# Eleven half-size products for twelve in the MLP's first matrix multiply, with shared parts added in PSUM

## The chip, the cores and the metric

The kernel runs on one core of one Trainium2 chip. The metric is the device time of one execution in microseconds. The five engines of a core are called PE (TensorE, matrix multiply), DVE (VectorE), ACT (ScalarE), POOL (GpSimd) and SP (SyncE, which here issues DMAs). Each works through its own instructions in order; they wait for each other through semaphores.

## The reference

A delta-rule attention makes tokens, and these go through an MLP with a hard-swish. All is fp32 in its results; the two MLP weights arrive as fp64.

```python
# attention: B, H, S, D = 4, 8, 768, 48
k_n = k / (norm(k) + 1e-6)
for t in range(S):
    y[:, :, t] = q_t @ state
    v_old = state^T k_t
    state = state + beta_t * outer(k_t, v_t - v_old)
# MLP: x is y as (B*S, H*D) = (3072, 384); w_in (384, 2048); w_out (2048, 384)
h = x @ w_in
g = h * np.clip(h + 3.0, 0.0, 6.0) / 6.0
return g @ w_out
```

## The kernel before

**Attention.** The sequence is cut into 24 chunks of 32 positions, for the 4 batches at once: 128 tokens a chunk. A chunk t has a preparation (`prep`, six chunks ahead: GpSimd normalises k into kb and makes the mask mb, PE transposes k and q, `pt`, and makes the scores, `sc`; DVE masks them into LB; GpSimd scales kb into bkb) and a chain (`chain`: state products `ks`, L775; R on DVE, L788; `pz`; the state's update `su`; the output `py`; the transposed output `yt`, which ACT copies into `xT`). Every four chunks a group of triangular matrices is inverted on DVE (`inverse`, L719 and L724: 60 small steps, each with two inputs in SBUF), and the norms of a later group are made (`norms`: GpSimd squares, DVE reduces).

**MLP.** Two chunks are a block of 256 tokens; there are 12 blocks. `up` makes x @ w_in for the 16 tiles of 128 features: three products of 128x128 weights with 256 token columns into one PSUM bank (L946), then ACT makes Relu(h/6 + 1/2) into a buffer t1 (L955) and DVE makes min(t1, 1) * h into g (L958). Block 0 is done in two halves of 128 columns, as each chunk's tokens arrive. Blocks 0 and 1 multiply by w_out plainly (`down`, L987). From block 2 on `down_by_seven` (L1052) uses Strassen's seven products, each of 8 feature tiles with 192 columns, done in two halves of four products. Its sums of g, 16 of 128x256 a block, are on DVE (L1038), spread over the products; the sums of w_out were made once.

**Order.** Nothing is scheduled by the tile framework; the code's own order is the order of each engine. Up to chunk 4 it is the list of words in `ORDER` (each word advances one generator by a step; `u` is a unit of the MLP, `i2` a step of an inverse). From chunk 5 on a loop gives each chunk 15 slots: in a slot come the chunk's planned steps, one MLP unit, then `settle`, which issues ACT's steps and all but one of DVE's final steps that are outstanding, then two or three steps of an inverse or of norms. A block has 14 units of `down_by_seven` and 16 of `up`, so two chunks' slots hold one block. After the last chunk the remaining MLP units run alone.

**Buffers.** PSUM has four banks shared by the MLP and the attention's small products (`psM`) and four for the chain (`psC`). kb has 2 buffers, bkb and LB 8, v 3, mb 2.

## Time and profile before

| | us |
|---|---|
| median of 3 runs (lowest, highest) | 699.43 (697.33, 704.33) |
| the profiled execution | 701.2 |
| its span | 699.5 |
| DVE, sums of g (L1038), 160 | 65.5 busy |
| DVE, final steps of 256 columns (L958), 176 | 73.3 busy |
| ACT, Relu of 256 columns (L955), 176 | 83.5 busy |
| GpSimd, mask steps of 128x256 (L423), 48 | 35.8 busy |
| chunk 7 begins (its `ks`), chunk 9 begins | 234.47, 286.44 |

A line of the profile names the source line, the engine, the operation and what it reads and writes (out<-in), with the partitions by the elements of a partition. PEld is the loading of weights into PE, which goes on beside PE's products. An fp32 product appears as two records of PE, and so does its weight load.

### The profile page before, as it was taken

How to read it: one execution, taken by the hardware profiler on the slowest of the kernel's cores; microseconds unless marked ns; L12 is line 12 of the kernel's file. 1: busy time of each engine (PE TensorE's matmuls, PEld its weight loads, DVE VectorE, ACT ScalarE, POOL GpSimd, SP SyncE). 2: the span in 40 equal slices, each digit the busy share in tenths (PEclk: the TensorE clock that was granted, in tenths of full speed). 3: DMA queues.
4: the chain of work that ended last, by engine and by line, in shares of the span. 5: the costliest groups of instructions: out<-in, count | busy, mean ns of one | idle time of the engine just before them, and what ended most of it. 6: DMA issues, size and time to landing. Idle time of an engine off the chain costs nothing.

```text
span 699.5 us, 25481 instructions
## 1 busy us (share of the span) xinstructions
PE 651.9 (93%) x11208; PEld 570.9 (82%) x11208; DVE 440.0 (63%) x1174; ACT 240.6 (34%) x476; POOL 93.5 (13%) x146
## 2 busy tenths in 40 slices
PE   2637779999999999999999999999999999999997
PEld 2437669777668998998998998988988989989997
DVE  5678737878545797653796743895544984545342
ACT  5786448722213313313213213223223132132230
POOL 7520110321321010411100401100000000000000
PEclk9857859999999999999999999999999999999999
DMA  6787777401513123414113422015130014000000
GB/s 134 213 195 196 115 210 173 67 33 20 104 39 80 34 43 70 48 39 88 32 29 78 45 45 65 10 42 78 18 70 2 2 36 59 16 11 1 24 0 23
DMA packets 137999, 45.27 MB, mean 65 GB/s; under 512 B 128192, under 2 KB 131264, under 8 KB 137888
## 3 DMA queue, kind: packets, MB, share of 16 engines
q1 hardware_dynamic: 137632, 43.35, 30.3%
q8 instruction: 88, 1.44, 0.9%
q10 hardware_dynamic: 256, 0.30, 0.2%
q14 instruction: 23, 0.19, 0.1%
HBM read 32.87 MB, written 10.75 MB: 62 GB/s over the span
## 4 chain that ended last, share of the span: by engine, by line
PE 81%; DVE 9%; DMA 4%; SPq 3%; issue 2%; ACT 1%; POOL 0%; DVEq 0%
PE ph L946 34%; PE po L1052 23%; PE po L987 6%; PE ks L775 3%; PE pt L474 3%; PE pz L796 3%; PE su L892 2%; PE py L796 2%; PE sc L495 2%; DVE A L724 2%; DVE pr L719 2%; SPq L147 2%; DVE g L1038 1%; DMA qb<-in_q_dram 1%; PE yt L841 1%
## 5 line engine op out<-in xcount | busy, mean ns | idle before, releaser
L946 PE MATMUL ph<-xT,w_in 128*128 128x256 f32 (+1 forms) x1248 | 269.5, 370 | 1.9 <-DVE g L958 1.7
L946 PEld LDWEIGHTS ph<-xT,w_in 128*128 128x128 f32 x1248 | 221.0, 193 | 31.3 <-DVE g L958 2.8
L955 ACT ACTIVATE t<-ph,halves 128x256 f32<-128x256 f32 (+1 forms) x208 | 94.5, 457 | 202.2 <-PE ph L946 201.0
L958 DVE SCALAR_TENSOR_TENSOR g<-t,ph 128x256 f32<-128x256 f32 (+1 forms) x208 | 81.9, 398 | 124.7 <-ACT t L955 124.4
L1052 PE MATMUL po<-w_out,g 128*128 128x192 f32 x640 | 113.3, 328 | 0.0
L1052 PEld LDWEIGHTS po<-w_out,g 128*128 128x128 f32 x640 | 103.8, 190 | 0.5
L1052 PE MATMUL po<-spare,g 128*128 128x192 f32 x480 | 84.8, 330 | 0.0
L1052 PEld LDWEIGHTS po<-spare,g 128*128 128x128 f32 x480 | 78.1, 190 | 1.8
L1038 DVE TENSOR_TENSOR g<-g 128x256 f32<-128x256 f32 x160 | 65.5, 462 | 0.5 <-PE po L1052 0.5
L724 DVE TENSOR_TENSOR A<-A,pr 128x30 f32<-128x30 f32 (+19 forms) x150 | 52.6, 351 | 3.7
L335 ACT ACTIVATE spare<-spare,places 128x768 uint16<-128x768 uint16 (+1 forms) x56 | 52.5, 941 | 4.1 <-DMA qb<-in_q_dram 2.3
L719 DVE TENSOR_TENSOR pr<-A 128x30 f32<-128x30 f32 (+19 forms) x150 | 49.7, 331 | 2.9
L423 POOL TENSOR_TENSOR mb<-beta_tok,mask 128x256 f32<-128x256 f32 x48 | 35.8, 769 | 104.0 <-DVE LB L505 103.9
L987 PE MATMUL po<-w_out,g 128*128 128x384 f32 x128 | 46.4, 501 | 0.0
L1059 ACT ACTIVATE o<-po 128x192 f32<-128x192 f32 x40 | 13.2, 331 | 88.5 <-PE po L1052 82.2
L482 ACT ACTIVATE KQ<-pt 128x512 f32<-128x512 f32 x48 | 28.5, 595 | 31.7 <-PE pt L474 30.4
L458 POOL TENSOR_TENSOR kb<-kf,inv 128x384 f32<-128x384 f32 x24 | 21.3, 888 | 113.4 <-PE pt L474 76.8
L845 ACT ACTIVATE xT<-yt 128x384 f32<-128x384 f32 x24 | 11.7, 488 | 64.7 <-PE yt L841 64.7
L987 PEld LDWEIGHTS po<-w_out,g 128*128 128x128 f32 x128 | 23.4, 192 | 12.6 <-issue 0.5
L474 PE MATMUL pt<-ident,kb 128*128 128x128 f32 x96 | 18.6, 328 | 15.8 <-POOL kb L458 15.8
L775 PEld LDWEIGHTS ks<-state,KQ 64*64 64x64 f32 x1472 | 25.1, 139 | 9.0 <-issue 6.6
L775 PE MATMUL ks<-state,KQ 64*64 64x48 f32 x1472 | 28.4, 225 | 2.5 <-issue 1.4
(104 smaller groups left out, 566.6 us busy)
## 6 DMA issues: line engine op xcount, KB each, us to landing
kf<-in_k_dram SPq DMA_DIRECT2D x96, 48.0 KB, 3.1
qb<-in_q_dram SPq DMA_DIRECT2D x96, 48.0 KB, 2.3
vf<-in_v_dram SPq DMA_DIRECT2D x96, 48.0 KB, 3.1
out_dram<-o SPq DMA_DIRECT2D x92, 48.0 KB, 1.6
spare<-in_moe_w_in_dram SPq DMA_DIRECT2D x4, 768.0 KB, 6.7
w_out<-in_moe_w_in_dram SPq DMA_DIRECT2D x4, 768.0 KB, 7.1
w_out<-in_moe_w_out_dram SPq DMA_DIRECT2D x4, 768.0 KB
spare<-in_moe_w_out_dram SPq DMA_DIRECT2D x4, 768.0 KB, 4.8
```

The lines of the kernel that those rows point to most:

```text
L335: nc.scalar.activation(out=z, in_=z if n else d.bitcast(I16)[:, :, :, 3], func=func, bias=places[:, n : n + 1], scale=scale,)
L423: nc.gpsimd.tensor_tensor(out=mb[:, e], in0=beta_tok[:, t, e:H:2].unsqueeze(2).unsqueeze(3).to_broadcast([P, NP, 2, C]), in1=mask2[:].unsq ...
L474: nc.tensor.transpose(pt[:, p, :], src[:, 2 * p : 2 * p + 2].rearrange("p e w -> p (e w)"), ident[:])
L719: nc.vector.tensor_tensor(out=pv, in0=A[:, j, j + 1 :].unsqueeze(1).to_broadcast([n, j, w]), in1=A[:, 0:j, j].unsqueeze(2).to_broadcast([n ...
L724: nc.vector.tensor_tensor(out=A[:, 0:j, j + 1 :], in0=A[:, 0:j, j + 1 :], in1=pv, op=ALU.subtract)
L775: nc.tensor.matmul(ph[y][c, e, D * p : D * p + D], lhsT=KQ[r, p * B // 2 + b // 2, 2 * y : 2 * y + 2, :].rearrange("k y c -> k (y c)"), rh ...
L946: nc.tensor.matmul(ph[:, cols], lhsT=w_in[:, s, f * 128 : (f + 1) * 128], rhs=xT[:, s, cols], start=(s == 0), stop=(s == NKT - 1),)
L955: nc.scalar.activation(out=t1, in_=ph, func=ACTF.Relu, bias=half, scale=1.0 / 6.0)
L958: nc.vector.scalar_tensor_tensor(out=g, in0=t1, scalar=1.0, in1=ph, op0=ALU.min, op1=ALU.mult)
L987: nc.tensor.matmul(pos[c][:], lhsT=gs[blk, f // 2][:, f % 2, c * P : (c + 1) * P], rhs=w_out[:, f, :], start=(f == 0), stop=(f == NFC - 1),)
L1038: nc.vector.tensor_tensor(out=A(f, *out), in0=A(f, *a), in1=A(f, *b), op=op)
L1052: nc.tensor.matmul(ps[n][:], lhsT=A(f - f % 2, *a)[:, f % 2], rhs=b[:, f], start=(f == 0), stop=(f == HF - 1),)
```

## The change

From block 2 on, `up` is replaced by `up_by_eleven`. It takes features two tiles at a time (a pair; 8 a block) and tokens in two halves of 128, and regards the first two of the three tiles of the inner dimension as a 2x2 matrix product, which it does in seven products (Winograd's form of Strassen); the third inner tile adds its four plain products. So a pair has eleven products of 128 columns in place of six of 256. The four results lie side by side in one PSUM bank. A first half (`begin`) does four products. Then ACT copies two of the four parts into g's tile (`aside`), and DVE makes three additions (`fork`), two of which write PSUM, so that shared parts stand in each place that needs them. A second half (`end`) adds seven products on top, and ACT and DVE make g from all 512 columns in one step each. Two pairs are in work at a time: the units are begin 0, begin 1, end 0, begin 2, end 1, and so on; `end` of a pair needs its `fork`.

The sums of w_in (S1, S2, S4, once, and W21 in place) and of x (four steps of 128x128 a block) are on GpSimd, and so are now the 16 sums of g of a block, which are issued in two groups of eight, after products 4 and 1. For room in SBUF, t1 is gone (Relu goes into g's tile), bkb and LB have 7 buffers, v 2, mb 1, and beta_tok keeps 8 of 32 columns. `ORDER` is a new list with 16 words `S` for the weight sums; it has 32 words `u` for 36 before. The last units are settled down to one outstanding step instead of two.

```diff
-    NKB, NQB, NBKB, NLB, NKQ = 2, 4, 8, 8, 7
+    NKB, NQB, NBKB, NLB, NKQ = 2, 4, 7, 7, 7
...
-    NVF = 3
+    NVF = 2
...
-        mb = mbs[t] = work.tile([P, 2, NP, 2, C], FP32, name="mb")
+        mb = mbs[t] = work.tile([P, 2, NP, 2, C], FP32, name="mb", bufs=1)
...
             def first(f=f, g=gs[blk, f // 2][:, f % 2, cols], ph=ph[:, cols], key=key):
-                t1 = mlp.tile([128, TB], FP32, name="t1", bufs=3)[:, cols]
-                nc.scalar.activation(out=t1, in_=ph, func=ACTF.Relu, bias=half, scale=1.0 / 6.0)
+                nc.scalar.activation(out=g, in_=ph, func=ACTF.Relu, bias=half, scale=1.0 / 6.0)
...
+    def weight_sums():
+        for j in range(0, NPR, 2):
+            r = slice(j, j + 2)
+            plus_minus(S1[:, r], W21[:, r], W22[:, r], ALU.add)
+            yield
+            plus_minus(S2[:, r], S1[:, r], W11[:, r], ALU.subtract)
+            yield
+            plus_minus(S4[:, r], W12[:, r], S2[:, r], ALU.subtract)
+            yield
+            needs(*(("used", n, f) for n in ("a", "b", "u") for f in range(2 * j, 2 * j + 4)))
+            plus_minus(W21[:, r], W11[:, r], W21[:, r], ALU.subtract)
+            yield
...
+    def token_sums(blk):
+        needs(("seam", blk * CB), ("seam", blk * CB + 1), ("up", blk - 1))
+        drain(gens["S"])
+        B11, B12, B21, B22, _, _ = x_tiles(blk)
+        plus_minus(T1x, B12, B11, ALU.subtract)
+        plus_minus(T2x, B22, T1x, ALU.subtract)
+        plus_minus(T4x, B21, T2x, ALU.subtract)
+        plus_minus(B12, B22, B12, ALU.subtract)
+        past.add(("sums", blk))
+
+    def up_by_eleven(blk):
+        needs(("sums", blk))
+        B11, T3x, B21, B22, B31, B32 = x_tiles(blk)
...
+        def begin(j):
...
+            mm(ph, 0, W11[:, j], B11, start=True)
+            mm(ph, 1, S1[:, j], T1x)
+            mm(ph, 2, W21[:, j], T3x)
+            mm(ph, 3, S2[:, j], T2x)
...
+            def aside():
+                nc.scalar.activation(out=gt[:, 0:2], in_=ph[:, 0:2], func=ACTF.Copy)
...
+            def fork():
+                nc.vector.tensor_tensor(out=gt[:, 2], in0=gt[:, 0], in1=ph[:, 3], op=ALU.add)
+                nc.vector.tensor_tensor(
+                    out=ph[:, 1:3], in0=ph[:, 1:3],
+                    in1=gt[:, 2].unsqueeze(1).to_broadcast([128, 2, P]), op=ALU.add,
+                )
+                nc.vector.tensor_tensor(out=ph[:, 3], in0=gt[:, 1], in1=ph[:, 2], op=ALU.add)
+                past.add(("fork", blk, j))
...
+        def end(j):
+            needs(("fork", blk, j))
+            ph = phs.pop(j)
+            mm(ph, 0, W12[:, j], B21)
+            mm(ph, 1, S4[:, j], B22)
+            mm(ph, 2, W22[:, j], T4x)
+            mm(ph, 0, W13[:, j], B31)
+            mm(ph, 1, W13[:, j], B32)
+            mm(ph, 2, W23[:, j], B31)
+            mm(ph, 3, W23[:, j], B32, stop=True)
...
+            def first():
+                nc.scalar.activation(out=g, in_=flat, func=ACTF.Relu, bias=half, scale=1.0 / 6.0)
+
+                def rest():
+                    nc.vector.scalar_tensor_tensor(
+                        out=g, in0=g, scalar=1.0, in1=flat, op0=ALU.min, op1=ALU.mult
+                    )
+                    read(("ph", blk, "by", j))
...
+        begin(0)
+        yield
+        begin(1)
+        yield
+        for j in range(NPR):
+            end(j)
+            yield
+            if j + 2 < NPR:
+                begin(j + 2)
+                yield
...
             for f in fs:
-                nc.vector.tensor_tensor(out=A(f, *out), in0=A(f, *a), in1=A(f, *b), op=op)
+                nc.gpsimd.tensor_tensor(out=A(f, *out), in0=A(f, *a), in1=A(f, *b), op=op)
...
         product(4, A22, T4, 1)
         copy(C21, 4, -1.0)
+        sums(ALU.add, A22, A21, A22, (*lo, *hi))
+        sums(ALU.subtract, A21, A11, A21, (*lo, *hi))
...
         product(1, A11, B11, 1)
         copy(u, 1)
-        sums(ALU.subtract, A21, A11, A21, lo)
+        sums(ALU.subtract, A11, A22, A11, (*lo, *hi))
+        sums(ALU.subtract, A12, A12, A11, (*lo, *hi))
...
+            last = (NFC if blk < FIRST else NFC - 2) - 3
+            for n, _ in enumerate(downs(blk)):
+                if n == last and UF <= blk + 1 < N // CB:
+                    token_sums(blk + 1)
+                yield
...
-                for n, _ in enumerate(up(blk + 1)):
+                for n, _ in enumerate((up_by_eleven if blk + 1 >= UF else up)(blk + 1)):
...
         for _ in units:
-            settle(2)
+            settle(1)
```

More of the change, by code (lines that the diff above doesn't have):

```diff
@@ L22 @@
 ORDER = """
-k*2 z k*2 B*2 k B*2 w q s*2 q n0 s q n0 s q z n0 s q s*2 k s z m0 k z*3 n0 k a c m1 k a k c q s a
-q*2 n0 n1 n0 q n0 p0 a n1 k*2 b0 p0 n1 c k*2 p0*2 k n1 k n1 p0 n1*2 w p1 n2 p0 w n2 b1 k p1 p0 k*2
-x0 p1 m2 p1 k n2 q p1 q n2 x0*2 n2 p1 q a n2 c n2 x0 n2*2 a c p2 a b2 p2 q*2 p3 a q*2 x0 b3 p3 n4
-q c p2 q p2 p3 q n4 x0 p2 q c q n4 p2 a n4 w n4*2 p3 n4 w p2 p4 a w x0 w b4 p4 p3 k c x0 p4 m3 k a
-k*2 a p1 p4 p3 p4 l2 x0 m4 a c a c a l1 p4 p3 a x0 p4 m5 a c l3 m6 a*2 c a l4 c k x0 c a k*2 x0 n5
@@ L28 @@
-k c x0 a k n5 a v x0 a c x0 v c a v x0 a i1 c v a v c w n5 c w a v n5 w c k*2 i1 h0 i1 k i1*2 h0 k
-i1*2 y0 i1*3 h0 y0 i1*2 k a y0 i1 c i1 y0 i1 a c a k i1*2 k h0 a i1 h1 a i1 c a k i1 k ua i1 y1 v
-c n5 v i1*2 ua ra v y1 a q i1 q i1 ua ga ra q i1 a i1 ua q ga i1*2 q ua ra i1 n5 x1 x2 i1 ra x3 ua
-ga x4 ra q ga n5 ga ua q h1 ra q ua ra q a ua q ga*2 ua q ra n5 ra q ua ra ga i1 ga n5 ua ga ra i1
-c a i1 ua i1 ga ua ra c q ra ua ra q a c q k ga a x1 ua k ga*2 x1 ra k x2 ra ga x2 x1 k u x2 x3 k
-ga x1 k c k x2 x1 k n5 n9 n5*2 k c v*2 n5 x4 x3 p5 x2 v n9 v h1 p6 x3 n9 v*2 n9 b6 k b5 k w*2 v p5
@@ L34 @@
-h1 v n9 v y1 p7 p5 n9 v*2 p6 y1 b7 k*2 c a y1 p8 c h1 y1 b8 p6 p8 a p7 w x3 h1 w a k a k*2 h2 x3 c
-k p7 k ub p8 h2 k p8 rb ub y2 k p8 gb c ub rb c a h2 gb rb y2 ub h2 k a gb k ub k ub rb k rb gb h2
-v rb gb a gb v k ub h2 a w k ub rb c k ub a k h3 gb k rb c k rb gb a ub v gb c v y2 rb a gb ub y2
-w a h3 ub rb ub rb gb v rb gb ub a v gb c ub v rb v h3 rb gb c a ub gb c h3 y2 rb u y2 gb y3 p6 a
-y3*2 p6 h3 y3 a y3 h3 p5 y3 q p5 u c q n9 q a c u q c q ru q a gu p5 q n9 q ru p6 p5 a u p6 m7 l5
-a gu l6 u a c m8 a p7 u q p7 c q c a q p7 q ru a p8 p7 u p8 m9 l7 n9 c l8 u ru m10 u gu*2 n9*2 u
@@ L40 @@
-n9*2 p9 i2 u ru b9 gu p10 p9 ru u b10 p9 gu p9 i2 x4 p9 i2*3 u i2*2 x4 i2 u i2*4 x4 i2 ru i2*2 h4
-x4 gu i2 u y4 i2 h4 u ru i2*2 y4 u i2*2 u gu i2*3 u ru i2 gu i2 u ru i2 gu i2 u i2*3 u i2*3 h4 ru
-i2 gu p9 h4 i2*2 y4 p9 u i2 p11 l9 y4 u ru i2 y4 gu u y4 i2*3 u i2*4 u ru i2 gu i2 u ru i2*3 gu u
-i2*4 u e i2*2 e*2 i2*3 u ru i2*2 gu i2 h4 ru e gu p10 h4 u p10*2 u p10 u i2*3 p10 u p10 l10
+k*2 z k*2 B*2 k B*2 w q s*2 q n0 s q n0 s q z n0 s k s*2 k s k z m0 z*2 k z a c k*2 a c q a q n0*2
+q n0*2 p0 n1 q a n1 q b0 p0 q n1 c q p0*2 k*2 n1 p0 n1*2 k n1 p1 p0 k*2 b1 p1 p0 w n2 x0 k m1 p1*2
@@ new lines @@
+k w p1 k n2 x0 k x0 n2 p1 q n2 x0 q x0 n2*2 x0 n2*2 q a c q n2 c p2 a q p3 a p2 b3 a q p3 x0 b2 q
+p2 q p2 n4 c q x0 p2 q n4 a p2 w c v n4 c w a w n4 w a n4*3 k x0 p4 k a p1 x0 k b4 p3 c p4 m2 x0
+l1 a p3 k p4*2 p2 p3 c m3 a p3 l2 c p4 a p4 p3 a x0 m4 l3 x0 a c a p4 a k x0 m5 l4 a k c x0 k a k
+c a k c a v c a c v*2 a c v a c i1 a c v w a x0 w h0 w n5 c q h0 q h0 n5 q i1 n5 q y0 i1 h0 q y0*2
+i1*2 n5 h1 y0 i1 q i1 a c i1 a i1 c a i1 k i1*2 a i1*3 a c y1 k i1 ua S a k i1 S k y1 a k S ua k
+i1 ra i1 k a ga ua k i1*2 k ua c ra*2 k i1 ua ra i1 k ga a i1 ua k i1 ga k ra i1 ua i1 k ra ga a
@@ new lines @@
+i1 ua k i1*2 ga x1 i1 x2 ga ua x4 ra c x3 k ra ua v ra a v ga*2 ua v ga ra v c ua ra v a ua ga v
+ga i1 u c ra*2 i1 ga n5 ga i1 h1 ua i1 q ua ra q ga ua ra c v ra q x1 q ga x1 ga q x2 x1 x2 q x3
+x1 x2 x3 x1 q x4 q n5 q c n5 w*2 n5 k n5 k n9 n5*2 x2 k n5 x3 k h1 x2 n9 k*2 n5 n9 p5 n9 p6 k c a
+b5 a p6 c b6 a p5 v h1 v p7 p5 y1 v w p6 b7 w a p8 p6 y1 a x3 c k*2 p6 p8 c k a y1 c k h1 k y1 w a
+k a ub h1 b8 x3 rb p7 c a h2 k gb k p7 c ub k a h2 k ub k rb k rb gb a gb h2 c p8 v ub v h2 p8 v
+rb ub p8 gb k ub k rb y2 gb k ub k rb y2 ub rb v n9 gb h2 w gb rb n9 a ub h2 a ub gb h3 c rb*2 a
@@ new lines @@
+gb ub c ub a gb h3 ub rb*3 gb v a gb ub v gb c h3 v rb a v gb p5 c y2 a q*2 c p5 q c q a ub q y2
+rb q y2 a gb q ub q y3 c rb p5 h3 y3 y2 y3 gb a c p6 y3 a p7 c y3 q a u q p5 q y3 m6 q a u l5 p7 c
+n9 p7 p6 ru u n9 m7 l6 gu n9*3 p8 ru p7 n9 m8 l7 u gu n9 p9 p8 u l8 m9 u p10 h3 ru b9 gu u h3 b10
+i2 p10 ru S h4 gu S*2 p9 h4 y4 u S p9 p10 y4 p9 i2 p10 p9 i2*2 u i2 p10 i2*4 u i2*4 u ru i2*2 gu u
+i2 ru i2 gu i2 p9 i2*2 x4 p9 u i2 m10 l9 x4 u i2*3 u ru i2*3 u ru S gu i2 S u i2 S*2 gu i2 u i2*2
+u ru i2*3 u ru gu i2*2 u gu i2*3 u i2*3 u ru i2*2 gu p10 ru S i2 S x4 gu S u x4 p10 S i2 l10 p11
@@ L44 @@
+h4 i2 u h4 i2 u i2*4 u ru i2*2 gu i2 u i2 ru i2*2 gu i2 u i2*3 u e*3 u ru gu e y4 ru S gu h4 y4 h4
+y4 i2 y4 i2*2
 """
@@ L183 @@
     spare = const.tile([128, 3, NFC // 2 * DM // 2], FP32, name="spare")
-    assert S <= spare.shape[2]
+    assert 2 * S <= spare.shape[2]
     beta_hm = spare[:, 2, 0:S]
@@ L206 @@
     parity = const.tile([P, 2, 2], FP32, name="parity")
-    beta_tok = persist.tile([P, N, C], FP32, name="beta_tok")
+    beta_tok = persist.tile([P, N, H], FP32, name="beta_tok")
     state = persist.tile([128, B, NP, D], FP32, name="state")
@@ L233, in settings @@
         yield
-        nc.vector.transpose(out=beta_tok[:].rearrange("p n h -> p (n h)"), in_=beta_hm)
+        turned = spare[:, 2, S : 2 * S]
+        nc.vector.transpose(out=turned, in_=beta_hm)
+        nc.vector.tensor_copy(
+            out=beta_tok[:], in_=turned.rearrange("p (n h) -> p n h", h=C)[:, :, 0:H]
+        )
         past.add("beta")
@@ L949, in up @@
                 )
+            past.add(("used", name, f))
             if f % 2 == 0 and not half_of:
@@ L953, in first @@
             def first(f=f, g=gs[blk, f // 2][:, f % 2, cols], ph=ph[:, cols], key=key):
-                t1 = mlp.tile([128, TB], FP32, name="t1", bufs=3)[:, cols]
-                nc.scalar.activation(out=t1, in_=ph, func=ACTF.Relu, bias=half, scale=1.0 / 6.0)
+                nc.scalar.activation(out=g, in_=ph, func=ACTF.Relu, bias=half, scale=1.0 / 6.0)
                 def rest():
                     nc.vector.scalar_tensor_tensor(
-                        out=g, in0=t1, scalar=1.0, in1=ph, op0=ALU.min, op1=ALU.mult
+                        out=g, in0=g, scalar=1.0, in1=ph, op0=ALU.min, op1=ALU.mult
                     )
@@ L970, in up, with w_tiles @@
             yield
+    UF = 2
+    NPR = NFC // 2
+    sums_in = const.tile([128, 3, NPR, P], FP32, name="sums_in")
+    S1, S2, S4 = (sums_in[:, i] for i in range(3))
+    def w_tiles(s, i):
+        return w_in[:, s].rearrange("p (j i c) -> p j i c", i=2, c=P)[:, :, i]
+    W11, W12, W21, W22 = w_tiles(0, 0), w_tiles(1, 0), w_tiles(0, 1), w_tiles(1, 1)
+    W13, W23 = w_tiles(2, 0), w_tiles(2, 1)
+    tsum = const.tile([128, 3, P], FP32, name="tsum")
+    T1x, T2x, T4x = (tsum[:, i] for i in range(3))
@@ new lines, in plus_minus @@
+    def plus_minus(out, a, b, op):
+        nc.gpsimd.tensor_tensor(out=out, in0=a, in1=b, op=op)
+    def weight_sums():
[10 more added lines that the diff above has]
+            yield
@@ new lines, in x_tiles @@
+    def x_tiles(blk):
+        x = xTs[blk]
+        return [x[:, s, i * P : i * P + P] for s in range(NKT) for i in range(CB)]
+    def token_sums(blk):
[7 more added lines that the diff above has]
+        past.add(("sums", blk))
@@ new lines, in up_by_eleven, with mm @@
+    def up_by_eleven(blk):
+        needs(("sums", blk))
+        B11, T3x, B21, B22, B31, B32 = x_tiles(blk)
+        phs = {}
+        def mm(ph, n, w, x, start=False, stop=False):
+            nc.tensor.matmul(
+                ph[:, n], lhsT=w, rhs=x, start=start, stop=stop, skip_group_check=True
+            )
+        def begin(j):
+            key = ("ph", blk, "by", j)
+            ring("pm", NPM, key)
+            ph = phs[j] = psM.tile([128, 4, P], FP32, name="ph", tag="pm")
+            mm(ph, 0, W11[:, j], B11, start=True)
+            mm(ph, 1, S1[:, j], T1x)
+            mm(ph, 2, W21[:, j], T3x)
+            mm(ph, 3, S2[:, j], T2x)
+            gs[blk, j] = mlp.tile([128, 2, TB], FP32, name="g", bufs=NFC // 2)
+            gt = gs[blk, j][:].rearrange("p i (t c) -> p (i t) c", c=P)
+            def aside():
+                nc.scalar.activation(out=gt[:, 0:2], in_=ph[:, 0:2], func=ACTF.Copy)
+            relus["u"].append(aside)
+            def fork():
[3 more added lines that the diff above has]
+                    in1=gt[:, 2].unsqueeze(1).to_broadcast([128, 2, P]), op=ALU.add,
+                )
+                nc.vector.tensor_tensor(out=ph[:, 3], in0=gt[:, 1], in1=ph[:, 2], op=ALU.add)
+                past.add(("fork", blk, j))
+            pending["u"].append(fork)
+        def end(j):
[8 more added lines that the diff above has]
+            mm(ph, 3, W23[:, j], B32, stop=True)
+            flat = ph[:].rearrange("p n c -> p (n c)")
+            g = gs[blk, j][:].rearrange("p i c -> p (i c)")
+            def first():
[3 more added lines that the diff above has]
+                        out=g, in0=g, scalar=1.0, in1=flat, op0=ALU.min, op1=ALU.mult
+                    )
+                    read(("ph", blk, "by", j))
+                pending["u"].append(rest)
+            relus["u"].append(first)
+            if j == NPR - 1:
+                past.add(("up", blk))
+        begin(0)
[8 more added lines that the diff above has]
+                yield
@@ L1073, in down_by_seven @@
         copy(C11, 2)
-        sums(ALU.add, A22, A21, A22, lo)
         yield
         product(1, A11, B11, 0)
-        sums(ALU.add, A22, A21, A22, hi)
         yield
@@ L1080, in down_by_seven @@
         copy(u, 1)
-        sums(ALU.subtract, A21, A11, A21, lo)
+        sums(ALU.subtract, A11, A22, A11, (*lo, *hi))
+        sums(ALU.subtract, A12, A12, A11, (*lo, *hi))
         yield
         product(5, A22, T1, 0)
-        sums(ALU.subtract, A21, A11, A21, hi)
         yield
@@ L1088, in down_by_seven @@
         add(C11, C11, u)
-        sums(ALU.subtract, A11, A22, A11, lo)
         yield
         product(7, A21, B12, 0)
-        sums(ALU.subtract, A11, A22, A11, hi)
         yield
@@ L1095, in down_by_seven @@
         copy(C12, 7)
-        sums(ALU.subtract, A12, A12, A11, lo)
         yield
         product(6, A11, T2, 0)
-        sums(ALU.subtract, A12, A12, A11, hi)
         yield
@@ L1127, in mlp_units, with downs @@
                 yield
-        for blk in range(1, N // CB):
-            if blk < FIRST:
-                for c in range(CB):
-                    for f in range(0, NFC, WF):
-                        if c == 0:
-                            needs(*(("read", ("ph", blk, f + i, None)) for i in range(2)))
-                        down(blk, c, f)
-                        yield
-            else:
-                yield from down_by_seven(blk)
+        def downs(blk):
+            if blk >= FIRST:
+                yield from down_by_seven(blk)
+                return
+            for c in range(CB):
+                for f in range(0, NFC, WF):
+                    if c == 0:
+                        needs(*(("read", ("ph", blk, f + i, None)) for i in range(2)))
+                    down(blk, c, f)
+                    yield
+        for blk in range(1, N // CB):
+            last = (NFC if blk < FIRST else NFC - 2) - 3
+            for n, _ in enumerate(downs(blk)):
+                if n == last and UF <= blk + 1 < N // CB:
+                    token_sums(blk + 1)
+                yield
             if blk + 1 < N // CB:
-                for n, _ in enumerate(up(blk + 1)):
+                for n, _ in enumerate((up_by_eleven if blk + 1 >= UF else up)(blk + 1)):
                     if blk + 1 == FIRST and n >= HF:
@@ L1221 @@
         a=scales(), c=rest, w=pieces(), q=queries(), v=values(), B=betas(), k=keys(), z=settings(), s=more_settings(),
-        ua=up(0, 0), ub=up(0, 1), u=mlp_units(),
+        S=weight_sums(), ua=up(0, 0), ub=up(0, 1), u=mlp_units(),
     )
@@ L1256 @@
             evicts.pop(0)()
+        drain(gens["S"])
         units = gens["u"]
```

## The prediction

> **What bounds the kernel now.** I read the profile's page first, then stretches of the span, TensorE's waits, and single stages in order of time.

> ```profile
> span 699.5 us, 25481 instructions
> PE 651.9 (93%) x11208; PEld 570.9 (82%) x11208; DVE 440.0 (63%) x1174; ACT 240.6 (34%) x476; POOL 93.5 (13%) x146
> PE   2637779999999999999999999999999999999997
> PE ph L946 34%; PE po L1052 23%; PE po L987 6%; PE ks L775 3%; PE pt L474 3%; PE pz L796 3%; PE su L892 2%; PE py L796 2%; PE sc L495 2%; DVE A L724 2%; DVE pr L719 2%; SPq L147 2%; DVE g L1038 1%; DMA qb<-in_q_dram 1%; PE yt L841 1%
> ```

> After the first 100 us TensorE is busy to the end, and the two matmuls of the MLP carry 63% of the last chain. A busy TensorE need not be at its peak, so I looked at stretches (columns: stretch, its length, busy time and count of PE, weight loads, DVE, ACT, POOL, clock, DMA share, GB/s) and at what PE waited for after 150 us (total, times, longest).

> ```profile
> 100.00:205.00 105.00, 104.67 (x1973) 79.55 (x1970) 74.59 (x179) 46.07 (x86) 22.92 (x28) 0.97 0.38 83
> 205.00:309.00 104.00, 103.43 (x1746) 93.36 (x1745) 72.08 (x191) 29.41 (x64) 15.98 (x20) 1.00 0.29 52
> ```

> ```profile
> PE ph L946 <- DVE g L958: 1.6, 3, 0.6
> ```

> The clock is full and PE waits 1.6 us in 550. So a TensorE pass saved is time saved, and a wait put on TensorE is time lost: no other slack takes it up.

> **The products.** Each fp32 product shows as two passes (11 blocks of 48 products give the 1056 records at 256 columns). Their pace is in the last block's chain, and that of a 128-column pass in the weight loads of block one, at full clock:

> ```profile
> 656.89 20.72 PE ph L946 x96
> 677.61 18.21 PE po L1052 x112
> ```

> ```profile
> 115.78 2.08 PEld L946 LDWEIGHTS ph<-xT,w_in 128*128 128x128 f32 x18
> 118.03 1.42 PEld L946 LDWEIGHTS ph<-xT,w_in 128*128 128x128 f32 x12 [0.16 <-DVE g L958]
> ```

> A 256-column pass: 20.72 / 96 = 0.2158 us. A 128-column pass, start to start: (2.08 - 0.19 of the last load) / 17 = 0.1112 us; half of 0.2158 would be 0.1079, so the loads stay hidden but for 3%. A pair of feature tiles had 6 products: 12 x 0.2158 = 2.590 us. It gets 11 of half the columns: 22 x 0.1112 = 2.446 us. That is 0.144 us a pair, and over 8 pairs and 10 blocks 11.5 us, not the 17 us that one product in twelve would give.

> [...]

> **ACT and DVE in the up stage.** The activations and DVE steps by form (line, engine, operation, shapes, count | busy us, mean ns):

> ```profile
> L958 DVE SCALAR_TENSOR_TENSOR g<-t,ph 128x256 f32<-128x256 f32 x176 | 73.3, 419 | 119.8 <-ACT t L955 119.5
> L1038 DVE TENSOR_TENSOR g<-g 128x256 f32<-128x256 f32 x160 | 65.5, 462 | 0.5 <-PE po L1052 0.5
> L958 DVE SCALAR_TENSOR_TENSOR g<-t,ph 128x128 f32<-128x128 f32 x32 | 8.6, 280 | 5.0 <-ACT t L955 4.9
> ```

> 419 against 280 ns gives 139 ns for 128 columns more, so 0.70 us for 512. DVE had 2 x 0.42 = 0.84 us a pair. It gets the three dependent additions of the fork, 0.28 + 0.42 + 0.28 with gaps of 0.03, so 1.06, and one last step of 0.70: 1.76 us. None of the trace's DVE rows writes PSUM; I take the row of the same size. ACT had 2 x 0.47 us; a copy of 256 lies between its rows at 192 (0.33) and 384 (0.49), so 0.38, and a Relu of 512 by its rows at 128 and 256 (0.36, 0.47) is 0.70: 1.08 us, hidden on an engine a third busy. Neither fills TensorE's 2.45 us, but the second half of a pair now waits on TensorE for ACT's copy and the whole fork: 0.26 us (as from the last pass of a group to ACT in the last block) + 0.38 + 0.05 + 1.06 + 0.05 = 1.8 us after the first half's four products. Behind that wait stand all later products, since TensorE takes its work in order. In the steady rhythm seven products of the pair before lie between (14 x 0.111 = 1.56 us) and the next first half (0.89): covered by 0.65 us. It is not covered in three places.

> **First pair of a block.** Only the second pair's first half (0.89 us) lies between. With two transposes of 0.60 each around it, and DVE's R steps (1.41, after the last addition to the output), the fork is ready about 0.2 us late: chunks 6, 10, 14. From chunk 18 there are no such transposes: 1.3 us each for two blocks, 0.9 in the last. Sum 4.1 us, bounds 0 and 8.

> **Chunks 9 and 13, with norms on DVE.** Three reductions in step with GpSimd's squares (1.49 us apart), R and a fourth stand before the last pair's final step, which product 4 reads: about 8.8 us after the chunk's start against 7.7 on TensorE. 1.1 us each, 2.2; bounds 0 and 7.

> **Chunks 7-8, 11-12, 15-16, 19-20, with an inverse on DVE.** Here GpSimd matters. What it does to DVE today:

> ```profile
> 244.93 1.42 POOL L423 TENSOR_TENSOR mb<-beta_tok,mask 128x256 f32<-128x256 f32 x2 [6.38 <-DVE LB L505]
> 245.03 1.59 DVE L1038 TENSOR_TENSOR g<-g 128x256 f32<-128x256 f32 x2
> 246.31 1.00 POOL L388 TENSOR_TENSOR sq<-kf 128x384 f32<-128x384 f32 x1
> 246.54 1.00 DVE L724 TENSOR_TENSOR A<-A,pr 128x210 f32<-128x210 f32 x1
> 247.58 0.39 DVE L719 TENSOR_TENSOR pr<-A 128x220 f32<-128x220 f32 x1
> ```

> Two DVE sums took 1.59 us for 0.75 otherwise, and a step of 0.38 took 1.00, while GpSimd ran: some 0.4 us lost for each GpSimd operation of 256 columns. So a sum moved (0.37 to 0.42 us of DVE) gives DVE nothing back where it has such steps queued. [...] The new fork and final steps have one input in PSUM, like L958.

> Today's backlog:

> ```profile
> 264.33 0.73 DVE L788 SCALAR_TENSOR_TENSOR R<-ks,parity,R 128x192 f32<-128x192 f32 x2
> 265.44 2.86 PE L946 MATMUL ph<-xT,w_in 128*128 128x256 f32 x12 [0.57 <-DVE g L958]
> ```

> R of chunk 8 ends at 265.06, 30.6 us after chunk 7 began (234.47). After the change DVE has in this stretch 16 sums less (seven pairs of 0.75 and that of 1.59, 6.8 us) and three final steps less (1.25); a fork and two final steps more (2.5), and 12 of 16 GpSimd sums that meet a two-SBUF step (4.8; the others meet steps on PSUM) and four token sums (0.8). Net 0: R again ends at 30.6, then two inverse steps (0.65) and the fork: 32.4. TensorE gets to the second half of the first pair after 13 half-products of 1.30, two second halves of 1.56, and 6.1 for the chunk's other matmuls (25.6 now, less 12 x 1.30 and 3 x 1.295), 26.1; then ks 1.15, a half-product 1.30, two transposes 1.2, two first halves 1.78: 31.5. So 0.9 us late, say 1.0; four times 4. Bounds: 0 if GpSimd's sums fall beside PSUM steps; 4.4 each if DVE is 3.5 us later (full blocking by every GpSimd operation).

> **GpSimd itself.** Its 256-column operation takes 0.61 to 0.66, so 16 sums a block 10 us (up to 13 in contention), beside 13 us of later products: A22 is due two products (5.2 us) after its four sums (2.5 to 3.1) may start, A12 by product 3, 7.8 us after the eight sums (4.9 to 6.2) may start. kb, mask and the four token sums (about 0.4 each) queue behind them; they end some 2.5 us before the next block's first products. That cover (product 3, ks) hides them; without it 1.6 us a block. Costed at nothing. The 16 weight sums (10 us, once) and the new written order come before 205 us, where PE is also full: 0, bounds -3 and +4. Narrower rings: v is loaded a chunk (25 us) ahead for a landing of 3.1, the mask waits for LB of the chunk before and is due a chunk later; on SP nothing moves past a tighter wait. Nothing.

> **Sum.** 701.2 us (the profiled execution; its span is 699.5) - 11.5 - 1.6 (today's waits) + 4.1 + 2.2 + 4 = 698.4. The median of the runs shown is 1.8 below that execution: 696.6, so 697.

> **The rivals.** First, all forks covered: DVE drops its sums and is ahead everywhere. For it speaks that DVE is 63% busy and free of inverse steps in most up stages; against it the 1.8 us path at each block's start. 701.2 - 13.1 + 2 - 1.8 = 688 to 690. Second, on the other side, DVE and GpSimd shut each other out in the inverse stretches, and TensorE, now tied to DVE twice a pair, waits for the whole backlog: 4 x 4.4 instead of 4, norms at 7, block starts 8, the early part +4: 701.2 - 13.1 + 36.6 - 1.8 = 723 at the very worst, 708 with six tenths of these waits (22 us). It decides from 20 us of them, 706.3. Third, the products cost more than 111 ns because every wait breaks the prefetch of a load (0.1 us, as seen when a group follows another kind): 16 halves x 10 blocks x 0.1 = 16 us, 713; but today's groups each begin with a wait already met, and keep 0.2158 throughout. Unlikely. That fewer columns are not streamed is excluded: a block has 88 half-size products for 48.

> **How the numbers follow.** The first has 0.28, the middle case 0.48, the second 0.20, the third 0.04. One per cent (7 us, about what can be told from no change) puts the bounds at 692.4 and 706.4. Range 688 to 709. Likeliest alone: 693 to 702.

> **What would show it.** Passes of the new products 0.111 apart; PE waits on DVE's fork at the first pair of each block, longest in chunks 8, 12, 16 and 20; DVE's inverse steps at 0.8 us beside GpSimd's sums; DVE's backlog before the up stages. A stretch of two blocks was 103 us; without waits it becomes 100.7. I am wrong if PE waits for GpSimd, for a ring, or in steady pairs.

## The result and the profile after

| | us |
|---|---|
| before, median of 4 runs | 699.61 |
| after, median of 4 runs (lowest, highest) | 726.66 (721.94, 730.74) |
| ratio (95% interval) | 1.0375 (1.0289 to 1.0462) |
| the profiled execution of after, its span | 728.45, 726.7 |

The changed kernel is 27 us slower; 697 was forecast, 688 to 709. From the page of after: the span, PE's and the clock's rows of slices, the chain's shares by engine and by line, and the two largest groups.

```profile
span 726.7 us, 27374 instructions
...
PE   2548688999999989999989999989999989999997
...
PEclk9656669999999989999989999989999999999999
...
PE 64%; DVE 13%; issue 13%; DMA 3%; ACT 2%; POOL 2%; SPq 2%; DVEq 0%; POOLq 0%; ACTq 0%
PE ph L1026 21%; PE po L1176 18%; PE po L1111 6%; PE ph L951 4%; DVE A L729 3%; DVE pr L724 3%; PE pt L479 3%; PE ks L780 3%; PE pz L801 2%; PE py L801 2%; PE su L897 2%; PE sc L500 2%; DVE R L793 1%; DVE g L1074 1%; DVE ph L1048 1%
...
L1026 PE MATMUL ph<-xT,w_in 128*128 128x128 f32 x1120 | 178.2, 284 | 17.1 <-DVE ph L1052 13.7
L1162 POOL TENSOR_TENSOR g<-g 128x256 f32<-128x256 f32 x160 | 119.4, 780 | 209.8 <-PE po L1176 176.8
```

PE's row, all nines from slice 7 in before, now has an 8 every six slices, in slices 15, 21, 27 and 33 (six slices are 109 us, two blocks); PEclk has it in the first three of them. In the chain PE has 64% where it had 81, DVE 13% for 9 and "issue" 13% for 2. The stretch shown of before, and PE's waits after 150 us (total, times, longest):

```profile
205.00:309.00 104.00, 99.13 (x1855) 91.87 (x1854) 76.11 (x185) 30.17 (x61) 39.16 (x54) 0.97 0.27 51
```

```profile
PE ph L1026 <- DVE ph L1052: 13.7, 9, 2.9
PE yt L846 <- DVE y L836: 2.2, 4, 1.0
PE ph L1026 <- ACT y L817: 2.1, 2, 1.0
PE po L1176 <- DVE g L1074: 1.5, 4, 0.4
PE ph L1026 <- DVE o L1186: 1.3, 3, 0.4
```

PE is busy 99.1 of 104 us for 103.4, at a clock of 0.97. The fork's last addition (L1052) ends the longest waits: 13.7 us in nine, where all waits of before came to 1.6. Four of the nine are 2.9 (three times) and 2.7 us, in chunks 8, 12, 16 and 20; the others 0.2 to 0.8. The first 2.9 in order of time, PE and VectorE:

```profile
264.39 0.35 DVE L1186 TENSOR_TENSOR o<-u,po 128x192 f32<-128x192 f32 x1
264.66 0.36 DVE L724 TENSOR_TENSOR pr<-A 128x198 f32<-128x198 f32 x1
264.80 0.49 PE L1026 MATMUL ph<-xT,w_in 128*128 128x128 f32 x2 [0.45 <-DVE o L1186]
265.05 0.37 DVE L729 TENSOR_TENSOR A<-A,pr 128x198 f32<-128x198 f32 x1
265.45 0.35 DVE L724 TENSOR_TENSOR pr<-A 128x184 f32<-128x184 f32 x1
265.72 0.73 DVE L793 SCALAR_TENSOR_TENSOR R<-ks,parity,vf 128x192 f32<-128x192 f32 x2
266.37 0.73 DVE L793 SCALAR_TENSOR_TENSOR R<-ks,parity,R 128x192 f32<-128x192 f32 x2
267.02 0.34 DVE L729 TENSOR_TENSOR A<-A,pr 128x184 f32<-128x184 f32 x1
267.39 0.33 DVE L724 TENSOR_TENSOR pr<-A 128x168 f32<-128x168 f32 x1
267.64 0.28 DVE L1047 TENSOR_TENSOR g<-g,ph 128x128 f32<-128x128 f32 x1
267.96 0.43 DVE L1048 TENSOR_TENSOR ph<-ph,g 128x256 f32<-128x256 f32 x1
268.43 0.30 DVE L1052 TENSOR_TENSOR ph<-g,ph 128x128 f32<-128x128 f32 x1
268.87 0.77 PE L1026 MATMUL ph<-xT,w_in 128*128 128x128 f32 x2 [2.91 <-DVE ph L1052]
```

VectorE works without a pause. Pair 0's four products were done before 264; its fork stands in VectorE's queue behind the last addition to the output, three inverse steps, R and two more inverse steps, and starts at 267.64. PE has issued pair 1's products (265.96 at the last) and stands for 2.9 us. The last line has another sign in it: two passes take 0.77 us for 0.49. In each of the three 2.9 us waits the granted clock falls to 0.5, for 6.83 us, and after the 2.7 us wait for 3.41 us: 23.9 us at half clock. Before, the clock is full from 106 us to 700.

Where the 27.2 us are, counting from the start of one PE product to the start of the next, by line (so waits and slow stretches count with the product before them): up stages of blocks 2 to 11 212.9 before, 226.2 after (+13.3); products of the down stages 187.2 and 193.0 (+5.8); pz and py from chunk 6 on 29.2 and 32.4 (+3.2). Chunk 5 begins at 182.1 for 183.5, but four units `u` of 1.3 us have been moved behind that point: +3.8. Sum 26.1.

### The profile page after: what moved, and what is told of

It is laid out like the page before. It is cut to its first block, busy times and chain, and to the rows that moved or that the text cites. A ratio compares the mean times of both kernels' runs of the same rounds, so it can differ in the third digit from the quotient of the medians.

```text
span 726.7 us, 27374 instructions
## 1 busy us (share of the span) xinstructions
PE 655.5 (90%) x12008; PEld 600.5 (83%) x12008; DVE 475.2 (65%) x1175; ACT 250.3 (34%) x476; POOL 239.6 (33%) x361
## 4 chain that ended last, share of the span: by engine, by line
PE 64%; DVE 13%; issue 13%; DMA 3%; ACT 2%; POOL 2%; SPq 2%; DVEq 0%; POOLq 0%; ACTq 0%
PE ph L1026 21%; PE po L1176 18%; PE po L1111 6%; PE ph L951 4%; DVE A L729 3%; DVE pr L724 3%; PE pt L479 3%; PE ks L780 3%; PE pz L801 2%; PE py L801 2%; PE su L897 2%; PE sc L500 2%; DVE R L793 1%; DVE g L1074 1%; DVE ph L1048 1%
## 5 line engine op out<-in xcount | busy, mean ns | idle before, releaser
L1026 PE MATMUL ph<-xT,w_in 128*128 128x128 f32 x1120 | 178.2, 284 | 17.1 <-DVE ph L1052 13.7
L1162 POOL TENSOR_TENSOR g<-g 128x256 f32<-128x256 f32 x160 | 119.4, 780 | 209.8 <-PE po L1176 176.8
L1026 PEld LDWEIGHTS ph<-xT,w_in 128*128 128x128 f32 x1120 | 151.1, 196 | 21.5 <-issue 12.6
L1071 ACT ACTIVATE g<-ph,halves 128x512 f32<-128x512 f32 x80 | 55.0, 687 | 122.8 <-PE ph L1026 72.6
L1074 DVE SCALAR_TENSOR_TENSOR g<-g,ph 128x512 f32<-128x512 f32 x80 | 54.8, 685 | 50.0 <-ACT g L1071 50.0
L724 DVE TENSOR_TENSOR pr<-A 128x30 f32<-128x30 f32 (+19 forms) x150 | 65.4, 436 | 3.4
L1026 PE MATMUL ph<-tsum,sums_in 128*128 128x128 f32 x320 | 61.9, 275 | 0.0
L1042 ACT ACTIVATE g<-ph 128x256 f32<-128x256 f32 x80 | 30.7, 383 | 72.3 <-PE ph L1026 72.3
L951 PE MATMUL ph<-xT,w_in 128*128 128x128 f32 (+1 forms) x288 | 49.5, 327 | 1.9 <-ACT KQ L487 1.0
L951 PEld LDWEIGHTS ph<-xT,w_in 128*128 128x128 f32 x288 | 43.0, 203 | 7.5 <-DVE g L963 1.3
L1026 PEld LDWEIGHTS ph<-tsum,sums_in 128*128 128x128 f32 x320 | 48.6, 192 | 0.0
L912 DVE TENSOR_TENSOR state<-state,su 128x384 f32<-128x384 f32 x46 | 23.3, 547 | 29.1 <-PE su L897 29.1
```

Of the source, the lines that this page charges most:

```text
L724: nc.vector.tensor_tensor(out=pv, in0=A[:, j, j + 1 :].unsqueeze(1).to_broadcast([n, j, w]), in1=A[:, 0:j, j].unsqueeze(2).to_broadcast([n ...
L951: nc.tensor.matmul(ph[:, cols], lhsT=w_in[:, s, f * 128 : (f + 1) * 128], rhs=xT[:, s, cols], start=(s == 0), stop=(s == NKT - 1),)
L1026: nc.tensor.matmul(ph[:, n], lhsT=w, rhs=x, start=start, stop=stop, skip_group_check=True)
L1042: nc.scalar.activation(out=gt[:, 0:2], in_=ph[:, 0:2], func=ACTF.Copy)
L1071: nc.scalar.activation(out=g, in_=flat, func=ACTF.Relu, bias=half, scale=1.0 / 6.0)
L1074: nc.vector.scalar_tensor_tensor(out=g, in0=g, scalar=1.0, in1=flat, op0=ALU.min, op1=ALU.mult)
```

## The experiments

Each is the kernel before or after with the part shown altered. A run of the kernel before on the same chip stands beside each. PE's waits are those of the profiled execution after 150 us.

| run | us | ratio (95%) | span |
|---|---|---|---|
| e1, sums of g on VectorE | 722.15 | 1.0364 (1.032 to 1.041) | 719.9 |
| e2, without 60 inverse steps | 704.43 | 1.0074 (1.005 to 1.010) | 703.7 |
| e3, before + sums of g on GpSimd | 706.05 | 1.0111 (1.010 to 1.013) | 704.2 |
| e4, after with the old up stage | 707.07 | 1.0125 (1.010 to 1.015) | 705.6 |
| e5, before + artificial pauses | 734.38 (one run) | - | 732.6 |
| e6, after with work in the wait | 722.64 | 1.0322 (1.029 to 1.035) | 717.1 |
| e7, after, inverse steps aside | 712.56 | 1.0178 (1.015 to 1.021) | 707.1 |
| e8, e4 with sums on VectorE | 705.00 | 1.0076 (1.004 to 1.011) | 703.0 |
| e9, e7 with sums on VectorE | 706.58 | 1.0087 (1.006 to 1.012) | 705.1 |
| e10, e9 with three pairs begun | 697.27 | 0.9966 (0.995 to 0.999) | 697.2 |
| e11, after with three pairs begun | 707.83 | 1.0120 (1.008 to 1.016) | 706.2 |
| e12, e1 with three pairs begun | 705.92 | 1.0078 (1.006 to 1.010) | 706.2 |

**Which part makes the loss: e1 to e4.** e1 puts g's sums back on VectorE, spread over the products as before:

```diff
-                nc.gpsimd.tensor_tensor(out=A(f, *out), in0=A(f, *a), in1=A(f, *b), op=op)
+                nc.vector.tensor_tensor(out=A(f, *out), in0=A(f, *a), in1=A(f, *b), op=op)
```

> The changed kernel with g's 16 sums per block back on DVE, spread over the products as before. Theory A (in the four blocks beside an inverse, GpSimd's sums hold up DVE's inverse steps, the first fork of the block comes 3 us late, and TensorE's clock then halves for 6.8 us: about 7 us a block, 28 us in all): R of chunk 8 ends again 31 to 33 us after chunk 7 begins (34.4 in the changed kernel), the wait falls to 1.5 us or less and the clock stays full: 704 to 712 us. Theory B (the waits come from the new up stage itself, whoever does the sums; DVE now has 6 us more per block): 724 us or more. Theory C (the written order, the rings and the weight sums): 724 to 729 us.

e2 leaves out the steps of the inverses of groups 3 to 6 (this part isn't computed):

```diff
-        for j in range(1, C - 1):
+        for j in range(1, C - 1 if g < 3 else 1):
```

> The changed kernel without the 60 DVE steps of the four inverses of groups 3 to 6 (their loads and stores stay; the output of chunks 9 to 23 is then not the reference's). Theory A: the four blocks lose their 7 us each: 696 to 702 us, no half-clock stretch after 120 us. Theory B: each block still waits at its first pair, at most 8 us gained: 718 us or more. Theory C: 722 us or more.

e3 is the kernel before with the `sums` of after: on GpSimd, in two groups of eight.

> The kernel before with only g's sums moved to GpSimd, in two groups of eight. Theory A: DVE's inverse steps take 0.8 us beside the sums here too and R of chunk 8 ends 3 to 4 us later, but the plain up stage needs DVE only to free PSUM: waits of 1 to 3 us in the three or four such blocks, 701 to 712 us. Theory B: no effect, 698 to 701 us. Theory C: 698 to 701 us.

e4 has the old up stage in all blocks, without weight and token sums; order, rings and GpSimd's sums are those of after:

```diff
-    UF = 2
+    UF = 99
```

> The changed kernel (its order, rings, GpSimd sums of g) with the plain twelve products in every block and without the sums of w_in and x. Theory A: as the kernel before with GpSimd sums, 701 to 712 us. Theory B: 698 to 702 us. Theory C: 715 us or more.

PE's waits in e1, then in e2:

```profile
PE ph L1026 <- DVE ph L1052: 16.2, 11, 3.4
PE ph L1026 <- DVE o L1186: 2.9, 3, 1.2
```

```profile
PE ph L1026 <- DVE ph L1052: 3.4, 8, 0.8
PE ph L1026 <- ACT y L817: 3.1, 3, 1.1
PE po L1176 <- DVE g L1074: 0.8, 2, 0.4
```

e1 is 4.5 us faster by the medians and 0.1% by the ratios, which the spread of the runs doesn't tell from nothing, and it keeps the long waits (2.92 three times, 3.35): the sums' engine hardly matters beside the new up stage. Counted from the trace, from each start to the next, VectorE has 41 inverse steps from the start of chunk 7 to the end of R of chunk 8 in both: 22.0 us and no sums in after, 15.7 us and 6.3 of sums in e1. In this stretch GpSimd takes from VectorE what it relieves it of. The first long wait of e1, on PE:

```profile
263.21 0.49 PE L1026 MATMUL ph<-xT,w_in 128*128 128x128 f32 x2 [1.20 <-DVE o L1186]
267.29 0.77 PE L1026 MATMUL ph<-xT,w_in 128*128 128x128 f32 x2 [2.92 <-DVE ph L1052]
```

Pair 1's first product waits for the last addition to the output, 1.20 us here and 0.45 in after. That wait takes up VectorE's lateness. The second is 2.9 us in both: it is what stands between the addition and the fork in VectorE's queue, less the products of pair 1.

e2 loses the long waits and all half-clock stretches, and 22 of the 27 us. What remains is 0.7% above before, though PE has less to do. In e3 the same GpSimd sums cost 7.6 us with the old up stage, by waits of 0.4 to 1.7 us. The new up stage alone (after against e4) costs 19.6.

**The clock: e5 and e6.** e5 puts a chain transpose, ACT copy, 1 to 10 GpSimd steps, transpose into the up stage of blocks 3 to 10 of the kernel before, so that PE stands for a chosen time with nothing else altered:

```diff
+            if f == 12 and blk in PAUSES:
+                pause(blk)
```

> The kernel before with one artificial wait of TensorE in the up stage of each of blocks 3 to 10: a small product, a copy on ACT, then 1, 2, 3, 4, 5, 6, 8 and 10 GpSimd steps of 128 columns (about 0.4 us each), and a product that waits for them. It measures the clock alone. If waits of about 3 us are what halves the clock: the waits grow from about 1.2 to 5 us, the clock stays full after the short ones (under 1.2 us as in the changed kernel) and falls to a half for 6.8 us after those of 2.9 us and more; the time is before's plus the waits (about 22 us) plus 3.4 us for each fall. If the half clock has another cause (the new products, the load of all engines): no fall at all, 699 plus the waits alone.

Waits of 1.10 and 1.58 us leave the clock full; after 2.06, 2.54, 3.49 and 4.45 it is 0.5 for 3.41 us, after 5.41 for 6.83; after 3.02 it stays full. The third pause by stretches of 3.41 us (columns as in the prediction's stretches):

```profile
382.17:385.58 3.41, 1.35 (x8) 0.93 (x7) 0.42 (x1) 0.92 (x3) 2.21 (x5) 1.00 0.30 51
385.58:389.00 3.42, 3.42 (x10) 2.65 (x9) 0.42 (x1) 0.47 (x1) 1.71 (x3) 0.50 1.47 125
389.00:392.41 3.41, 3.41 (x19) 3.03 (x18) 0.84 (x2) 1.55 (x4) 0.00 (x0) 1.00 0.79 101
```

PE is idle 2.06 of the first 3.41 us and pays in the second. All changes of the clock in this trace lie on one grid of 3.413 us. The wait of 3.02 us lies across a grid line, 1.3 us on one side and 1.8 on the other. e1's longest, 3.35 us, lies across one with 1.6 and 1.8, and the clock stays full there too. So what counted in these two runs is the idle part of one such window.

e6 does four products of pair 1 three times in blocks 3, 5, 7 and 9, 1.8 us of work where PE would stand:

```diff
-            mm(ph, 0, W11[:, j], B11, start=True)
+            for _ in range(3 if j == 1 and blk in (3, 5, 7, 9) else 1):
+                mm(ph, 0, W11[:, j], B11, start=True)
```

> The changed kernel with the first half of pair 1 done three times over in blocks 3, 5, 7 and 9 (the last time counts): 1.8 us of needless products put where TensorE waits 2.9 us for the first fork. Theory A (the wait itself is DVE's and stays, but the half clock after it comes from TensorE's idleness): the wait shrinks to about 1.1 us, no half-clock stretch is left, and the needless work costs nothing: 716 to 720 us. Theory D (the half clock is not due to the wait, or costs nothing): 725 to 730 us, falls stay.

The same stretch in after, then in e6:

```profile
263.00:275.00 12.00, 8.64 (x167) 7.81 (x166) 9.72 (x31) 3.71 (x7) 0.00 (x0) 0.72 0.22 51
```

```profile
263.00:275.00 12.00, 10.83 (x206) 10.39 (x207) 11.13 (x34) 3.72 (x8) 1.97 (x3) 1.00 0.31 62
```

The waits fall from 2.9 to 1.1 by the work put in, and the clock stays full from 99 to 716 us. PE does 7 us more and the span is 9.6 us shorter. Of this 1.7 us are there at the start of chunk 5, before any of the long waits (180.4 for 182.1). In the four chunks with the long waits, start to start, e6 gains 2.4, 2.4, 2.7 and 1.6 us: in these two traces the half clock cost about 9.0. In the timed runs the gain is 4.0 (726.66 to 722.64), with a spread of 5 to 9 us in each. The granted clock is listed per run as a mean only: in after 0.960 for the run of 721.94 us, as in the runs of the kernel before (0.956 to 0.970), and 0.941 to 0.948 for the other three (724.88 to 730.74). So it seems that the fastest run met few half-clock stretches or none; how many each met isn't shown.

**The early part and the queue: e7 to e9.** e7 keeps the inverse steps out of six slots around the first pair and adds them elsewhere:

```diff
-                if i == 1 and 5 < u < 12:
+                if i == 1 and 5 < u < 9 or i == 2 and u > 11 or i == 3 and u < 3:
                     continue
-                take(fill, 2 + (u % 3 == 0))
+                take(fill, 2 if i in (1, 3) and u > 2 else 2 + (u % 3 == 0))
```

> The changed kernel with the inverse's steps kept out of the six slots around the first pair of the block (slots 12 to 14 of the third chunk of a group and 0 to 2 of the fourth); in their place two steps a slot from slot 9 of the second chunk and from slot 3 to the end of the fourth. The work is the same. Theory A, in the form that the first pair's fork stands in DVE's queue behind a backlog of inverse steps: some 10 to 12 steps of 0.4 to 0.5 us leave the way, the waits of 2.9 us fall below 0.6 us, the clock stays full, and a few waits of under 1 us appear in the later pairs: 704 to 712 us. Theory E (DVE has too much to do in the two chunks, wherever it stands): the waits move to the later pairs, 718 us or more.

e8 is e4 with g's sums on VectorE: the order, the rings and Relu into g's tile are all that is left of the change.

> The changed kernel with the plain twelve products, without the sums of w_in and x, and with g's sums on DVE: what is left of the change is its written order, the narrower rings and Relu into g. From the start of chunk 5 in the run with plain products (1.6 us earlier than before, though 5.2 us of products were moved behind it) the order costs 3.6 us: 702 to 704 us. If that loss was GpSimd's: 698 to 700 us.

e9 is e7 with g's sums on VectorE.

> As the run with the steps kept aside, with g's sums on DVE. By the first experiment a moved sum gives DVE as much as GpSimd's collisions take: within 4 us of that run (theory A). If the collisions are worse once the steps stand elsewhere: 5 us or more faster.

e7 takes the first pair's waits in the inverse blocks to 0.4 and 1.0 and gives back 14 us; e9 gives back 20. e8 costs 5.5 us for nothing but order and rings; its trace has no wait after 150 us but one of 1.4, and 2.7 us in two between 119 and 128 that before has not:

```profile
PE sc L500 <- issue: 1.7, 1, 1.7
PE ph L951 <- ACT KQ L487: 1.0, 1, 1.0
```

The second is a copy queued on ACT behind conversions of the weights. In the first, scores are next in line while VectorE, after such conversions, still has to empty the bank of the scores before. Both are in after (1.8 and 1.0). e9 against e8 is the new up stage without long waits: no gain, 706.58 against 705.00.

**The order of two half-pairs: e10 to e12.** In all three pair 2 is begun before pair 0 is ended:

```diff
         begin(1)
         yield
+        begin(2)
+        yield
         for j in range(NPR):
             end(j)
             yield
-            if j + 2 < NPR:
+            if 0 < j and j + 2 < NPR:
```

> The kernel of e9 (sums on VectorE, inverse steps kept out of the slots around the first pair) with one line of the new up stage moved: the first four products of pair 2 are issued before pair 0 is ended, so that TensorE has 0.45 us more work of its own between pair 0's first products and its last seven. Theory A (what is left over in e9 is TensorE standing at the start of every up stage for the first fork, 0.32 us in blocks up to eight and 1.0 us in the later ones, 6.2 us over eleven waits): the 0.32 waits go, the 1.0 waits fall to about 0.55, and the span falls from 705.1 to about 701.5, the ratio from 1.0087 to about 1.004; still no gain over the kernel before, since the early part costs 3 to 4 us more there. Theory B (the up stage is slow through its order and its banks, not through that first wait): the waits move to the second pair or to the banks, and the span stays at 704 to 706.

> The changed kernel itself (sums on GpSimd, inverse steps where they were) with only the one line of e10 moved: pair 2's first four products before pair 0 is ended. Theory A (in the inverse blocks the fork stands behind the last add, three inverse steps, R and two more steps in VectorE's queue, 2.9 us of them; 0.45 us more of TensorE's own work cannot cover that): the four waits go from 2.9 to about 2.4 us and the clock still falls to half after most of them; the other blocks lose their waits of 0.4 to 1.0 us and what lies behind them, 0.6 to 1.3 us a block as e10 showed; the span falls from 726.7 to 716 to 721, the ratio to 1.024 to 1.033. Theory B (the lead of two pairs was the whole fault, the inverse steps only its occasion): the waits of the inverse blocks go as in e10, the clock stays full, and the ratio falls to 1.01 or less.

> The changed kernel with two parts altered: g's sums on VectorE (as e1) and pair 2's first four products before pair 0 is ended (as e11); the inverse steps stay where they were. With e11 (ratio 1.012), e10 (0.9966) and e9 it splits what is left. Theory A (whose engine does the sums matters little, as e1 showed with 4.5 us; the rest of the 10 us between e11 and e10 is the inverse steps beside the first pair): 703 to 705 us, ratio 1.005 to 1.008. Theory B (the sums on GpSimd are what is left of the loss, since without the long waits their collisions are no longer hidden behind them): 697 to 700 us, ratio 0.997 to 1.002.

PE's waits in e10, then in e11, then e12:

```profile
PE po L1178 <- DVE g L1074: 1.1, 3, 0.4
PE ph L1026 <- DVE ph L1052: 0.7, 2, 0.5
```

```profile
PE ph L1026 <- DVE ph L1052: 2.7, 6, 0.9
PE yt L846 <- DVE y L836: 2.6, 4, 1.3
PE ph L1026 <- DVE o L1188: 1.4, 3, 0.5
PE po L1178 <- DVE g L1074: 1.1, 3, 0.4
```

```profile
PE ph L1026 <- DVE ph L1052: 3.0, 7, 0.9
PE ph L1026 <- DVE o L1188: 2.8, 3, 1.2
```

e11 is the changed kernel with this alone: 18.8 us come back, and nothing is at half clock between 132 us and the end of the products. The expectation of theory A (1.024 to 1.033) was too high, since it counted only the 0.45 us of the products moved. What PE does in e11 where it stood in after:

```profile
265.93 0.39 PE L1026 MATMUL ph<-xT,w_in 128*128 128x128 f32 x2
266.15 0.39 PE L1026 MATMUL ph<-tsum,sums_in 128*128 128x128 f32 x2
266.37 0.39 PE L1026 MATMUL ph<-xT,w_in 128*128 128x128 f32 x2
266.60 0.39 PE L1026 MATMUL ph<-tsum,sums_in 128*128 128x128 f32 x2
267.06 1.03 PE L801 MATMUL pz<-R,LB 32*32 32x48 f32 x64
268.02 0.86 PE L500 MATMUL sc<-KQ 64*32 64x64 f32 x64
268.92 0.49 PE L1026 MATMUL ph<-xT,w_in 128*128 128x128 f32 x2
```

Pair 2's four products, then pz and sc, which belong to the next slot and which `end(0)` had stood in front of; the seven products follow at 268.92. The fork's last addition runs at 268.57 here and at 268.43 in after: VectorE is as late as it was, and PE has something to do meanwhile.

In e12 theory A (703 to 705 us) came within 1 us and B (697 to 700) fell: with three pairs begun, GpSimd's sums cost 1.9 us against VectorE's (e11 to e12, with overlapping intervals), the inverse steps beside the first pair 8.7 (e12 to e10). e10 is the only kernel below the one before, by 0.3%. By PE's starts its up stages take 202.8 us, of the 11.5 us expected of the products 10.1; most of that it pays again before chunk 5, which begins 0.6 us later than before with 5.2 us of units still to do. An order without these early waits was not run.

## Why the prediction was wrong

- **Products, −11.5.** The pace is right: 0.111 us a pass also in the loads of the new lines, and e10 gets 10.1. e2, without long waits but with the short ones, gets 1.9 (211.0 for 212.9).
- **First pair of a block, 4.1.** Right in place and near in size: 0.3 and 0.4 (for 0.2) in chunks 6, 10 and 14, 1.0 (for 1.3) twice and 0.8 (for 0.9). The fork itself took 1.09 us (267.64 to 268.73) for 1.06.
- **Chunks 9 and 13, 2.2.** 0.4 us of wait each: too high.
- **Inverse blocks, 4 × 1.0.** This is the step that failed: the waits are 2.9 three times and 2.7, 11.5 in all. "Net 0: R again ends at 30.6" after chunk 7 began; it ended at 34.4. VectorE begins the chunk five inverse steps behind (41 in the stretch for 36): 1.9 us at before's 0.377 a step. Two additions into w_out of 0.55 us (L1152) are in this chunk, which before had done earlier; chunks 11 and 15 have none, and R ends 34.0 us after they begin. The collisions with GpSimd took 6.5 (22.0 for 41 steps) for the 5.6 charged, and the sums gone from VectorE freed 6.2 and not 6.8. GpSimd itself is not what made R late: in e1, with the sums on VectorE, R ends at 34.2. So the fork ended 36.0 us after chunk 7 began and not 32.4, while PE came to it at 33.2 and not 31.5, 1.1 of it in three small waits (0.33, 0.29, 0.45). The wait is 2.9 and not 0.9, inside the bounds (0 to 4.4). The upper bound of 4.4, which the second rival takes four times, supposes that VectorE stands for the whole of each GpSimd operation (0.61 us); no run shows that: 22.0 less e1's 15.7, over 16 sums, is 0.39 a sum, and 0.45 in the stretches of chunks 11 and 15 (22.3 less 15.2), while a GpSimd sum took 0.86 (median of the 16 from 342 to 376 us).
- **No term for the clock.** This is the other half of the failed step: the sum priced a wait at its length. Each of these four also brought 3.4 or 6.8 us at half clock: 9.0 us by e6. The waits and the clock together, 11.5 + 9.0 = 20.5, are about what e2 (22) and e11 (19) give back. Of the 30 us between the sum's 698.4 and the profiled 728.45 they make 16.5 (20.5 for 4.0); with the order's 3.8 some 10 are left, which aren't split further.
- **Order, 0 (−3 to +4).** +3.8 in the trace, at the upper bound; e8 puts order and rings together at 5.5. In the traces of the runs that share this early part chunk 5 begins between 180.3 (e7) and 184.5 (e12), so the 3.8 is good to about 2 us. The rings were not run apart from the order.
- **GpSimd's sums, rings, token sums.** No wait of PE after 150 us names them. But nothing was won: in the inverse stretches the sums moved gave VectorE nothing back, as forecast, and with the old up stage they cost 7.6 us (e3).
- **The rivals.** The second (VectorE and GpSimd shut each other out in the inverse stretches, 708 to 723) had the place and the sign; TensorE did wait for VectorE's backlog, but not because GpSimd and VectorE shut each other out, since the long waits stay with the sums on VectorE (e1). What decides is PE's order against VectorE's queue: e11 moves one half-pair and the waits go, with VectorE's lateness unchanged. The third fell: at full clock the passes keep their 0.11 us, and what waits break costs about 0.1 us at a group's start (two passes from 264.80 take 0.32 us to the next start, for 0.22).

Not settled: how the gain of e11 divides between wait and clock in undisturbed timed runs, since only one execution of each kernel is profiled.

## What to carry to other kernels

When a step makes the matrix engine depend on the vector engine in the middle of a product, look at what stands in front of it in the vector engine's queue at the worst place, and put independent matrix work of the same length ahead of the dependent one in the matrix engine's own order; one half-pair moved was worth 19 us here. Price a wait of more than about 1.7 us on a full matrix engine with the clock that it may cost: here 1.7 us of idling in one window of 3.41 was followed by 6.8 us at half. Before moving sums to GpSimd, look at what the vector engine does meanwhile: here its inverse steps, with two operands in SBUF, took 22.0 us beside the moved sums, as much as steps and sums together in e1.

## What the runs showed of the hardware

VectorE's steps with two inputs in SBUF often lost time beside GpSimd's: in before a sum of g (L1038) has a median of 0.42 us and takes up to 1.06, and the inverse step of 0.38 took 1.00. Steps with an input in PSUM kept their time: the final steps of before (L958) have a median of 0.42 us and a longest of 0.42, and the fork's additions of after 0.28, 0.43 and 0.30 with none more than 0.01 us longer.
